# Retention and gated MLP on one core: state sums in SBUF for two chunks at a time, a two-step norm, other staging and a new order of the steps

## The chip, the cores and the metric

The kernel runs on 1 core of one Trainium2 chip. The metric is the device time in microseconds (us) of one execution; lower is better. The engines are TensorE (PE, with its weight loads shown as PEld), VectorE (DVE), ScalarE (ACT), GpSimd (POOL) and SyncE (SP, which here only issues DMAs). Each engine works through its own instructions in order; engines wait for each other by semaphores.

## The reference

Attention without softmax, with a decay that depends on the distance (retention), is followed by a gated MLP block whose gate mixes along the sequence (a 576 x 576 matrix `w_sg`). Batch 8, 8 heads, sequence 576, head size 64, model width 512, `d_ff` 1024.

```
scores = scale * q @ k^T
ret    = scores * where(rel >= 0, gamma_h ** rel, 0)      # per head
x      = (ret @ v) with the heads side by side             # [8, 576, 512]
h      = gelu_tanh(x @ w_in);  u, v = halves of h          # 512 columns each
v_n    = (v - mean(v)) / sqrt(var(v) + 1e-6) * g_ln
v_s    = w_sg @ v_n (along the sequence) + b_sg
out    = x + (u * v_s) @ w_out
```

## The kernel before

The 8 x 576 = 4608 rows are cut into 18 blocks j of 256 rows, each of two chunks of 128 rows, c or t = 0 and 1. In the attention part a block is held with two neighbouring rows on one partition: 64 partitions are chunk 0, 64 are chunk 1. Half of one chunk in nine belongs to the next batch (`m == MID`); there the states begin anew.

The whole program is one list of words, `ORDER`, written out by hand or by a tool; each word calls one step, and the steps are recorded in that order. Because every engine works in order, this list sets what stands ahead of what on PE, DVE, ACT, POOL and in SP's queue. A letter at the end of a word (A, D, P) gives the engine of an evacuation or a cast. A PSUM tag (x0, x1, w, y, z) gives the bank that a step writes; a step waits until the earlier content of its tag has been read. The steps, with their names in the list and in the trace:

- `ld:j:part` loads q, k or v of a block (`qf`, `kf`, `vf`), 512 KB each; `ldw` loads a weight, `ldg` the gain `g_ln`. All go through SP's queue.
- `cast` makes bf16 of them: `qb` = q times the decay of its row (two halves, L302), `kb` (two halves), `vb` = v times the inverse decay (L309).
- `T` transposes q or k on PE (`tp`, eight transposes, L327), `Te` copies the result to `qT` or `kT`. For 15 of the 36 a DMA transpose does it (`Td`).
- `Sc:j:g` makes the scores inside a chunk for half of the heads (`sc`, L350), `Sce` masks them (`ret`, DVE, L360).
- `Z:j:c` adds k^T v of one chunk to the state, in PSUM (`zp`, L382; 16 matmuls of 64 x 64): the running sum stays in one PSUM tile of a pool of its own (`psZ`) from one start of a batch to the next. `Ze` copies the sum to bf16 (`zb`), which later chunks read.
- `inter:j` and `intra:j` give the block's output (`ot`, L419): `ot<-qT,zb` from the states, `ot<-ret,vb` within the chunk. `intrae` copies it to `xT`, a ring of 9 blocks. Matmuls of 64 x 64 use one quarter of PE's array each; matmuls of different quarters run side by side.
- `V:j` makes the second half of h (`hv`, L454), `Ve` its GELU (`vg`); `mom` the mean and variance on DVE; `pow` the inverse root (`rs`) on POOL; `cen` on DVE `vc = (vg - mean) * g_ln` in one SCALAR_TENSOR_TENSOR (L484); `norm` `vn = vc * rs` on ACT, POOL or DVE (L498, L500; the chunk with two batches into two tiles `vnm`, always on ACT, L493).
- `U:j:x` and `Ue` make the first half of h (`hu`, L509; `uT`). `W:b:c:x` multiplies with the transposed `w_sg` (`wp`, L523), `We` multiplies with `uT` to `gT` (L528). `wT` and `wTe` are the transposes of `w_sg` for it; `sg` casts its rows to bf16 first, into a free part of `uT`.
- `O:j:t` multiplies with `w_out` (`op`, L535). The residual x is either added on PE (four matmuls with the identity, L538) or, for the six blocks with a word `xd` (a DMA transpose of `xT` to `xn`), by DVE in `Oe` (L547). `Oe` otherwise copies (`ob`), `st` stores.

Of the kernel before, what the change touches and what calls it, by code (L numbers as in the profile page):

```python
# [13 lines left out]
I32 = mybir.dt.int32  # L14
# [14 lines left out]
wTe:8:A ld:4:v:0 U:2:0:x0 cast:4:q:P norm:0:0:A T:4:q:x1 Ue:2:0 ld:4:v:1 Sce:3:1 Ze:3:1:A intra:3 mom:2:0 intrae:3:A cast:4:k:P ld:5:k Te:4:q:D
cen:1:0 norm:0:1:A cen:1:1 U:1:0:w norm:1:0:A T:4:k:x1 V:3:b:z Te:4:k:D ld:5:v Sc:4:0 U:2:1:x1 bd:0 Ue:1:0 pow:2:0 Ve:3:b cast:5:q:P mom:2:1  # L30
norm:1:1:A T:5:q:x0 Sce:4:0 cast:4:v:P ld:6:k:1 Te:5:q:A inter:4 Sc:4:1 U:3:0:w W:0:0:0:0:x0 Sce:4:1 intra:4 Z:4:1 mom:3:0 ld:6:q:1 Ue:2:1 cast:5:k:P
ldw:out ld:6:q:0 Ue:3:0 T:5:k:w intrae:4:A U:3:1:x1 cen:2:0 cen:2:1 V:4:b:z norm:2:0:A Te:5:k:D cast:5:v:P ld:6:v:1 Ue:3:1 Ze:4:1:D W:0:0:0:1 Sc:5:0
mom:3:1 ld:6:k:0 We:0:0:0 Z:5:0 Sce:5:0 Ze:5:0:A Ve:4:b W:0:3:0:2:w cast:6:q:P ld:7:q wc:out:A W:0:1:1:2:x1 ld:6:v:0 We:0:3:0 W:0:2:0:2:x0 We:0:2:0
inter:5 We:0:1:1 Sc:5:1 W:0:1:0:2:w W:0:2:1:2:x0 W:0:3:1:2:x1 Sce:5:1 We:0:2:1 We:0:1:0 intra:5 cast:6:k:P pow:2:1 Z:5:1 We:0:3:1 ld:7:k intrae:5:A
U:4:1:w T:6:q:x0 V:5:b:z cen:3:0 Ue:4:1 Ze:5:1:A cen:3:1 cast:7:q:P T:6:k:x1 mom:4:0 U:5:1:w ld:7:v Te:6:q:A W:0:0:1:0:x0 Te:6:k:A U:5:0:x1 Sc:6:0
norm:2:1:P cast:6:v:D mom:4:1 Z:6:0 Ve:5:b W:0:0:1:1 cast:7:k:P Ue:5:1 O:0:0:w We:0:0:1 Sce:6:0 mom:5:0 pow:3:b Ue:5:0 Ze:6:0:A O:1:1:x0 Z:6:1 inter:6
norm:3:0:D ld:8:q cast:7:v:P Td:7:q Oe:1:1:A Sc:6:1 Sce:6:1 ld:8:k Oe:0:0:A O:0:1:x0 norm:3:1:A T:7:k:x1 ld:8:v cen:4:1 mom:5:1 Ze:6:1:A Te:7:k:A
U:4:0:w bd:1 ld:9:q intra:6 Ue:4:0 Sc:7:0 pow:4:b intrae:6:A Z:7:0 Oe:0:1:A ld:9:k O:1:0:x1 cen:5:1 cen:4:0 ld:10:k Sce:7:0 V:6:b:z Ze:7:0:D
cast:8:k:A Ve:6:b cast:8:q:P pow:5:b Oe:1:0:A U:6:1:x0 norm:4:0:D T:8:k:w inter:7 Te:8:k:D Sc:7:1 cast:8:v:P Z:7:1 Sce:7:1 T:8:q:x1 Ue:6:1 cen:5:0
st:0 Ze:7:1:A W:1:3:0:2:w ld:9:v W:1:2:0:2:x0 Te:8:q:A We:1:2:0 intra:7 Sc:8:0 cast:9:k:P Z:8:0 norm:4:1:A Td:9:k W:1:0:1:2:x1 We:1:3:0 W:1:0:0:2:w  # L40
ld:11:k:0 W:1:1:0:2:x0 mom:6:0 We:1:0:1 norm:5:0:A We:1:0:0 intrae:7:A U:7:0:x1 Ue:7:0 V:7:b:z We:1:1:0 Ve:7:b O:2:1:x1 mom:6:1 cast:10:k:P ld:10:q
Oe:2:1:A Ze:8:0:D Sce:8:0 cast:9:q:P ld:11:q:0 mom:7:0 cast:9:v:P ld:10:v W:1:3:1:2:w inter:8 Sc:8:1 We:1:3:1 norm:5:1:P ld:11:q:1 Sce:8:1 mom:7:1
T:9:q:x1 U:6:0:w W:1:1:1:2:x0 We:1:1:1 Te:9:q:A Z:9:0 Ue:6:0 cen:6:1 cen:6:0 intra:8 intrae:8:A Sc:9:0 pow:6:b W:1:2:1:2:x1 norm:6:0:D cast:10:q:P
U:7:1:w V:8:b:z norm:6:1:A W:2:3:0:2:x0 pow:7:b Ue:7:1 Td:10:k We:1:2:1 Sce:9:0 ld:11:k:1 Ve:8:b Ze:9:0:A ld:11:v:1 cen:7:0 W:2:0:0:2:x1 U:8:1:w
cast:10:v:P We:2:3:0 Z:9:1 inter:9 Sc:9:1 Ue:8:1 mom:8:0 W:2:0:1:2:x0 T:10:q:w ld:13:k:1 We:2:0:0 Sce:9:1 norm:7:0:A Te:10:q:D W:2:3:1:2:x1 Ze:9:1:A
intra:9 st:1 Sc:10:0 Z:10:0 W:2:1:1:2:w We:2:3:1 We:2:0:1 Ze:10:0:A O:3:0:x1 intrae:9:A mom:8:1 cast:11:q:P ld:11:v:0 pow:8:b Sce:10:0 cast:11:k:A
We:2:1:1 cen:7:1 O:3:1:x0 V:9:b:z cen:8:1 Td:11:q U:8:0:w Oe:3:1:A Oe:3:0:A cen:8:0 Ve:9:b W:2:2:1:2:x1 norm:7:1:A mom:9:0 norm:8:0:P inter:10 Z:10:1
Sc:10:1 Ue:8:0 We:2:2:1 Ze:10:1:A O:2:0:x0 Oe:2:0:A W:2:2:0:2:x1 Sce:10:1 norm:8:1:P Td:11:k W:3:0:1:2:w W:2:1:0:2:x0 ld:12:q ld:13:q:0 intra:10
# [44 lines left out]
def kernel(  # L93
# [510 lines left out]
```

## Time and profile before

| | |
|---|---|
| time, median of 3 runs | 218.66 us (218.62 to 219.58) |
| the profiled execution: its own time | 218.48 us |
| its span, first to last instruction | 216.7 us |
| busy: PE, PEld, DVE, ACT, POOL | 194.7, 136.8, 170.3, 123.3, 122.1 us |
| instructions: DVE, ACT, POOL | 289, 179, 144 |
| granted TensorE clock | 1.00 |
| HBM read, written | 33.05 MB, 9.44 MB |

Busy time of an engine is the time in which at least one of its instructions runs. The matmul spans on PE overlap, so a step's cost there is read from start to start. In a row of groups stand line, engine, operation, out<-in with shapes and types, the count, then busy us and mean ns of one, then the engine's idle time just before them and what ended most of it.

### The profile page before, as it was taken

To read this page: it belongs to the slowest core of one execution; us is meant where nothing else is said; L and a number is where in the kernel's file an instruction comes from. 1 tells how busy PE (TensorE), PEld (TensorE's weight loads), DVE (VectorE), ACT (ScalarE), POOL (GpSimd) and SP (SyncE) were. 2 spreads that over 40 slices of the span, in tenths; PEclk is the share of its full clock that TensorE was granted. 3 is DMA by queue.
4 is the path that set the end of the run, shared out by engine and by line. 5 is a ranking of instruction groups with operands and counts; after the bars stand their busy time and mean duration, and the time that the engine had idled before them with its cause. 6 is when DMAs were issued, how large, how long until landed. Compare 5 with 4: busy or idle time off the path is not lost.

```text
span 216.7 us, 7228 instructions
## 1 busy us (share of the span) xinstructions
PE 194.7 (90%) x3101; PEld 136.8 (63%) x3130; DVE 170.3 (79%) x289; ACT 123.3 (57%) x179; POOL 122.1 (56%) x144
## 2 busy tenths in 40 slices
PE   0468788899999989999999999999999999999993
PEld 0355566577677657686667767686756675666751
DVE  3666858988995899799977678797988887977770
ACT  3356475697868578567563477833674457633102
POOL 5055338889169996988368565659729422151000
PEclk9999999999999999999999999999999999999999
DMA  6999999998999999999779899999899999450755
GB/s 168 290 343 355 222 233 263 208 226 190 290 217 254 208 247 324 197 249 174 184 172 282 180 263 252 217 207 254 128 269 230 265 238 271 141 149 3 191 198 194
DMA packets 86704, 48.47 MB, mean 224 GB/s; under 512 B 24528, under 2 KB 79824, under 8 KB 86672
## 3 DMA queue, kind: packets, MB, share of 16 engines
q1 hardware_dynamic: 86560, 48.00, 96.7%
q8 instruction: 24, 0.39, 0.8%
q14 instruction: 8, 0.07, 0.1%
q10 hardware_dynamic: 112, 0.00, 0.0%
HBM read 33.05 MB, written 9.44 MB: 196 GB/s over the span
## 4 chain that ended last, share of the span: by engine, by line
PE 63%; DVE 16%; DMA 12%; ACT 2%; issue 2%; SPq 1%; POOL 1%; DVEq 0%; ACTq 0%; POOLq 0%
PE wp L523 14%; PE op L535 12%; DMA vf<-in_v_dram 12%; PE hv L454 11%; PE hu L509 10%; PE ot L419 5%; DVE ret L360 5%; PE sc L350 3%; DVE vc L484 3%; PE zp L382 2%; DVE bst L468 2%; PE op L538 2%; DVE vn L500 2%; PE wtp L279 2%; PE tp L327 2%
## 5 line engine op out<-in xcount | busy, mean ns | idle before, releaser
L360 DVE TENSOR_TENSOR ret<-sc,mask 128x1024 bf16<-128x1024 f32 x36 | 43.8, 1216 | 5.8 <-PE sc L350 5.6
L302 POOL TENSOR_TENSOR qb<-qf,gq 128x512 bf16<-128x512 f32 x30 | 32.7, 1109 | 22.1 <-DMA qf<-in_q_dram 20.7
L523 PE MATMUL wp<-wT,vn 128*128 128x288 bf16 x256 | 40.8, 286 | 0.1
L509 PE MATMUL hu<-xT,w_in 128*128 128x256 bf16 x288 | 36.8, 273 | 0.0
L535 PE MATMUL op<-w_out,gT 128*128 128x512 bf16 x126 | 35.0, 380 | 1.2 <-issue 0.3
L528 DVE TENSOR_TENSOR gT<-wp,uT 128x288 bf16<-128x288 f32 x64 | 28.0, 449 | 9.8 <-PE wp L523 8.2
L454 PE MATMUL hv<-w_in,xT 128*128 128x512 bf16 x133 | 34.0, 382 | 1.6 <-ACT xT L137 0.8
L137 ACT CAST xT<-ot 128x1024 bf16<-128x1024 f32 x17 | 22.3, 1311 | 17.8 <-PE ot L419 17.7
L484 DVE SCALAR_TENSOR_TENSOR vc<-vg,mv,g_bc 128x512 f32<-128x512 f32 x36 | 31.5, 897 | 0.2
L514 ACT ACTIVATE uT<-hu 128x512 bf16<-128x512 f32 x36 | 21.3, 599 | 16.7 <-PE hu L509 16.4
L509 PEld LDWEIGHTS <-w_in 128*128 128x128 bf16 x288 | 27.1, 98 | 5.0
L523 PEld LDWEIGHTS <-vn 128*128 128x128 bf16 x256 | 24.6, 98 | 8.0 <-issue 0.4
L309 POOL TENSOR_TENSOR vb<-vf,gv 128x1024 bf16<-128x1024 f32 x13 | 25.1, 1934 | 7.2 <-DMA vf<-in_v_dram 5.5
L468 DVE BATCH_NORM_STATS2 bst<-vg 128x6 f32<-128x512 f32 x36 | 24.6, 683 | 4.5 <-ACT vg L461 4.5
L461 ACT ACTIVATE vg<-hv 128x1024 f32<-128x1024 f32 (+1 forms) x19 | 18.6, 980 | 13.2 <-PE hv L454 11.6
L500 POOL TENSOR_SCALAR vn<-vc,rs 128x512 bf16<-128x512 f32 x12 | 20.6, 1720 | 9.3 <-DVE vc L484 9.2
L454 PEld LDWEIGHTS <-xT 128*128 128x128 bf16 x144 | 13.5, 99 | 14.7 <-ACT xT L137 1.4
L137 ACT COPY ob<-op 128x512 f32<-128x512 f32 x20 | 11.5, 586 | 18.5 <-PE op L538 17.8
L477 POOL TENSOR_SCALAR rs<-mv 128x2 f32<-128x2 f32 (+1 forms) x19 | 8.1, 427 | 23.8 <-DVE mv L469 22.8
L535 PEld LDWEIGHTS <-gT 128*128 128x128 bf16 x144 | 12.9, 98 | 11.6
L523 PE MATMUL wp<-wT,vnm 128*128 128x288 bf16 x64 | 18.0, 287 | 0.3 <-DVE kT L137 0.3
L350 PE MATMUL sc<-qT,kT 64*64 64x128 bf16 x576 | 16.3, 223 | 0.8 <-DVE ret L360 0.6
(74 smaller groups left out, 283.2 us busy)
## 6 DMA issues: line engine op xcount, KB each, us to landing
out_dram<-ob SPq DMA_DIRECT2D x16, 512.0 KB, 4.6
kf<-in_k_dram SPq DMA_DIRECT2D x12, 512.0 KB, 7.6
qf<-in_q_dram SPq DMA_DIRECT2D x12, 512.0 KB, 6.6
vf<-in_v_dram SPq DMA_DIRECT2D x12, 512.0 KB, 8.1
gT<-in_moe_w_in_dram SPq DMA_DIRECT2D x2, 1024.0 KB, 9.5
qf<-in_q_dram SPq DMA_DIRECT2D x4, 384.0 KB, 8.2
kf<-in_k_dram SPq DMA_DIRECT2D x4, 384.0 KB, 8.3
vf<-in_v_dram SPq DMA_DIRECT2D x4, 384.0 KB, 8.5
```

The costliest lines, as they stand in the source:

```text
L137: (nc.scalar.copy if eng == "A" else ENG[eng].tensor_copy)(o, i)
L302: ENG[eng].tensor_tensor(s["qb"][:, a], paired(x)[:, a], g, op=Alu.mult)
L309: ENG[eng].tensor_tensor(s["vb"][:].rearrange("p a h d -> p h a d"), x[:], bc(gv, j), op=Alu.mult)
L360: nc.vector.tensor_tensor(s["ret"][:, :, 2 * g:2 * g + 2].rearrange("p r x a t -> p r x (a t)"), PS.pop(("Sc", j, g))[:].rearrange("p r x ...
L454: nc.tensor.matmul(hv[:, n], xT[:, (2 * j + t) % (2 * RING), kk, :], w_in[:, kk, F2:], start=(kk == 0), stop=(kk == KK - 1))
L468: nc.vector.bn_stats(bst[:], s["vg"][:, t])
L484: nc.vector.scalar_tensor_tensor(s["vc"][:, t], s["vg"][:, t], s["mv"][:, t, 0:1], g_bc[:], op0=Alu.subtract, op1=Alu.mult)
L500: ENG[eng].tensor_scalar(vn[:], vc[:, t], rs[:, t:t + 1], None, op0=Alu.mult)
L509: nc.tensor.matmul(hu[:, i, :], w_in[:, kk, 128 * c:128 * c + 128], xT[:, c0:c0 + 2, kk, :], start=(kk == 0), stop=(kk == KK - 1), skip_gr ...
L523: nc.tensor.matmul(PS["W", b, c, x][:], vns[t0 + j][e][:, 128 * c:128 * c + 128], wT[:, e, j, x * HS:(x + 1) * HS], start=(j == 0), stop=( ...
L528: nc.vector.tensor_tensor(gT[:, c, col:col + HS], PS.pop(("W", b, c, x))[:], uT[:, c, col:col + HS], op=Alu.mult)
L535: nc.tensor.matmul(op[:], gT[:, c, 128 * i:128 * i + 128], w_out[:, c, :], start=(c == 0), stop=(c == KK - 1 and not turn), skip_group_che ...
```

## The change

**States.** `psZ` is gone; its bank becomes a fourth rotating tag (v) beside x0, x1 and w. `Z:j:0` only takes a PSUM slot; `Z:j:1` then issues the matmuls of both chunks, interleaved, each chunk into its own slot (in 14 blocks; blocks 4, 8, 13 and 17 have one state addition, as before). `Ze` no longer copies a running sum: it adds the chunk's product from PSUM to the sum of the chunk ahead, f32 in SBUF (`zs`), always on DVE (24 words), or copies it where a state begins (8 words). A new word `Zc` casts `zs` to `zb`: 12 on ACT, 5 on DVE, 15 on POOL.

**Norm.** For blocks 0 to 15, `cen` and `norm` are replaced by `xh` and `gm`. `pow` makes one more small value per chunk on POOL (`mr` = -mean * rs). `xh` makes the normalised row, `vc = vg * rs + mr`, as one ACT activation with two per-row operands (30 words), or on DVE (2); `gm` multiplies with `g_ln` to `vn`, a TENSOR_TENSOR of two SBUF operands, 17 on DVE and 15 on POOL (two halves for the chunk with two batches). Blocks 16 and 17 keep `cen` and `norm`.

**Staging.** The bf16 rows of `w_sg` go to tiles that share the buffers of `ob` and `xn` (`wpad`), no longer to `uT`; the last 64 rows of `w_sg` are loaded by a word of their own (`s5`). Some small tables share buffers too.

**Head.** `fill:n:tag` puts n matmuls of zeros (128 x 512) on PE: ten words, 33 matmuls, the last ahead of `intra:1`.

**End.** The last unit, `O:17:1`, is computed, copied and stored in two halves of 256 columns (`Oh`, `Oeh`, `sth`).

**Turns and order.** T words 21 to 23, `Td` 15 to 13, `xd` 6 to 8 blocks; all words stand in a new order, with other engines for many evacuations and casts. Words per engine (before to after): `Oe` ACT 20 to 16, DVE 16 to 19; `Te` ACT 12 to 14, DVE 9 and 9; q casts DVE 3 to 5, POOL 15 to 13; k casts ACT 7 to 9, DVE 2 to 0; `intrae` ACT 17 to 15, DVE 1 to 3; `wTe` ACT 4 to 6, DVE 6 to 4.

The core of the diff (of the list the first line alone):

```
-ld:0:k rl ld:0:q ld:0:v cast:0:k:D ld:1:k T:0:k:x1 ld:1:q mk:0 cast:0:q:D Te:0:k:A T:0:q:x1 cast:0:v:D Z:0:0 Te:0:q:A Ze:0:0:A mk:1 Sc:0:0 Z:0:1
+warm rl ld:0:q ld:0:k cast:0:q:P ld:0:v fill:10:v T:0:q:x0 cast:0:k:A mk:0 T:0:k:v ldw:v cast:0:v:D ld:1:q mk:2 mk:1 Te:0:q:A ld:1:k Te:0:k:A spare
...
-    psZ = ctx.enter_context(tc.tile_pool(name="psZ", bufs=1, space=bass.MemoryType.PSUM))
...
+    def fill(n, tag):
+
+        o = ps2("idle", [128, 4, 128], tag)
+        for _ in range(n):
+            nc.tensor.matmul(o[:], zeros[:], zeros[:].unsqueeze(1).to_broadcast([128, 4, 128]), start=True, stop=True,
+                             skip_group_check=True)
...
+    def Z_mm(j, c, tag):
+
+        s = blk[j]
+        PS["Z", j, c] = ps2("zp", [128, KK, D], tag)
+        if c == 0 and (2 * j + 1) % NT != NT - 1:
+            return
+        for part in (False, True):
+            rows = [[], []]
+            for c in range(2):
+                if ("Z", j, c) not in PS or ((2 * j + c) % NT == MID) != part:
+                    continue
+                lo = slice(64 * c + (32 if part else 0), 64 * c + 64)
+                for a in range(2):
+                    for kk in range(KK):
+                        for r in range(2):
+                            rows[c].append((r, 64, lambda z=PS["Z", j, c], lo=lo, a=a, kk=kk, r=r: nc.tensor.matmul(
+                                z[half(r), kk, :], s["kb"][lo, a, kk, r, :], s["vb"][lo, a, hd(r, kk), :],
+                                start=(a == 0 and kk == 0), stop=True, skip_group_check=True)))
+            interleave(rows)
...
+    def Z_out(j, c, eng):
+
         i = 2 * j + c
...
+        sums[i] = w2.tile([128, KK, D], F32, name="zs")
+        z = PS.pop(("Z", j, c))
+        if opens(i):
+            move(eng, sums[i][:], z[:])
+        else:
+            nc.vector.tensor_tensor(sums[i][:], z[:], sums[i - 1][:], op=Alu.add)
+
+    def Z_cast(j, c, eng):
+        i = 2 * j + c
+        zbs[i + 1] = w3.tile([128, KK, D], BF, name="zb")
+        move(eng, zbs[i + 1][:], sums[i][:])
...
+        if j < NB - 2:
+            for t in tiles(t):
+                nc.gpsimd.tensor_scalar(blk[j]["mr"][:, t:t + 1], blk[j]["mv"][:, t, 0:1], blk[j]["rs"][:, t:t + 1], -1.0,
+                                        op0=Alu.mult, op1=Alu.mult)
+
+    def unit(j, t, eng):
...
+            nc.scalar.activation(s["vc"][:, t], s["vg"][:, t], Act.Identity, bias=s["mr"][:, t:t + 1],
+                                 scale=s["rs"][:, t:t + 1])
...
+    def gain(j, t, eng):
...
+            ENG[eng].tensor_tensor(vn[:], vc[:, t], g_bc[:], op=Alu.mult)
```

How the list moves the instructions is shown at three places. First SP's queue, from its first DMA on; a tile's name is followed by the array it is loaded from. Before:

```order
L158 DMA kf<-in_k_dram 128x8x128
L158 DMA qf<-in_q_dram 128x8x128
L158 DMA vf<-in_v_dram 128x8x128
L158 DMA kf<-in_k_dram 128x8x128
L158 DMA qf<-in_q_dram 128x8x128
L201 DMA gT<-in_moe_w_in_dram 128x4x512
L158 DMA vf<-in_v_dram 128x8x128
L201 DMA gT<-in_moe_w_in_dram 128x4x512
L201 DMA gT<-in_moe_w_sg_dram 128x4x576
```

SP's queue now, from its first DMA on:

```order
L160 DMA qf<-in_q_dram 128x8x128
L160 DMA kf<-in_k_dram 128x8x128
L160 DMA vf<-in_v_dram 128x8x128
L223 DMA gT<-in_moe_w_in_dram 128x4x512
L160 DMA qf<-in_q_dram 128x8x128
L160 DMA kf<-in_k_dram 128x8x128
L160 DMA vf<-in_v_dram 128x8x128
L160 DMA kf<-in_k_dram 96x8x128
```

q stands ahead of k in block 0, one half of `w_in` ahead of block 1, and all of block 1 ahead of the other half; the second half of `w_in` has moved behind block 2 and `w_sg` behind block 3.

Second DVE in the first block, from the v cast (`vb`) to the second masked score (`ret`). Before:

```order
L309 TENSOR_TENSOR vb<-vf,gv 128x8x2x64
L246 TENSOR_SCALAR mask_137<-rel 128x256
L249 MEMSET mask_137 32x4x16
L360 TENSOR_TENSOR ret<-sc,mask_136 128x2x512
L246 TENSOR_SCALAR mask_138<-rel 128x256
L249 MEMSET mask_138 32x4x16
L360 TENSOR_TENSOR ret<-sc,mask_136 128x2x512
```

DVE now, from the masks of the first block to the q cast of the second; `zs` is the state's f32 sum:

```order
L267 MEMSET mask_135 32x4x16
L139 COPY zs<-zp 128x256
L378 TENSOR_TENSOR ret<-sc,mask_134 128x2x512
L418 TENSOR_TENSOR zs<-zp,zs 128x256
L378 TENSOR_TENSOR ret<-sc,mask_134 128x2x512
L320 TENSOR_TENSOR qb<-qf,gq 128x512 x2
L139 CAST xT<-ot 128x8x2x64
```

The state's copy and its sum, one of them on ACT before, stand ahead of the two `ret`; a q cast and the copy to `xT`, on POOL and ACT before, stand behind them.

Third POOL in the middle, around the casts of blocks 7 and 8. Before:

```order
L137 CAST kb<-kf 128x512 x2
L477 TENSOR_SCALAR rs<-mv 128x2
L478 TENSOR_TENSOR rs<-rs,mhalf 128x2
L309 TENSOR_TENSOR vb<-vf,gv 128x8x2x64
L477 TENSOR_SCALAR rs<-mv 128x2
L478 TENSOR_TENSOR rs<-rs,mhalf 128x2
L302 TENSOR_TENSOR qb<-qf,gq 128x512 x2
```

POOL now, around the same casts; `vn<-vc,g_bc` is a gain product, `zb<-zs` a state's cast:

```order
L139 CAST kb<-kf 128x512 x2
L327 TENSOR_TENSOR vb<-vf,gv 128x8x2x64
L535 TENSOR_TENSOR vn<-vc,g_bc 128x512 x2
L139 CAST zb<-zs 128x256
L320 TENSOR_TENSOR qb<-qf,gq 128x512 x2
L327 TENSOR_TENSOR vb<-vf,gv 128x8x2x64
L139 CAST zb<-zs 128x256
```

Two gain products and two state casts have come between the input casts of block 7 and those of block 8; each state cast waits for what stands ahead of it.

More of the change, by code (lines that the diff above doesn't have):

```diff
@@ L29 @@
[L29 to L36, printed above, removed]
@@ L364, in Sc_out, with opens @@
             op=Alu.mult)
-    zcur = [None]
-    def Z_mm(j, c):
+    def opens(i):
+        return i % NT in (0, MID)
+    def Z_mm(j, c, tag):
         s = blk[j]
-        i = 2 * j + c
-        m = i % NT
-        first = m in (0, MID)
-        if first:
-            zcur[0] = psZ.tile([128, KK, D], F32, name="zp")
-        z = zcur[0]
-        lo = slice(64 * c + (32 if m == MID else 0), 64 * c + 64)
-        rows = [[], []]
-        begun = set()
-        def mm(a, kk, r):
-            h = hd(r, kk)
-            nc.tensor.matmul(z[half(r), kk, :], s["kb"][lo, a, kk, r, :], s["vb"][lo, a, h, :],
-                             start=(first and r not in begun), stop=True, skip_group_check=True)
-            begun.add(r)
-        for a in range(2):
-            for kk in range(KK):
-                for r in range(2):
-                    rows[c].append((r, 64, lambda a=a, kk=kk, r=r: mm(a, kk, r)))
-        interleave(rows)
-        PS["Z", j, c] = z
```

187 lines of the change are left out of this document (121 added, 66 removed).

## The prediction

> **What bounds the kernel now.** I read first the busy times by stage (length; then busy time and count of PE, PE weight loads, DVE, ACT, POOL; granted clock; DMA share; GB/s):
>
> ```profile
> 0.00:15.00 15.00, 4.61 (x84) 3.42 (x85) 8.07 (x23) 6.83 (x10) 5.01 (x18) 1.00 0.94 263
> 15.00:45.00 30.00, 25.17 (x483) 18.16 (x486) 22.47 (x36) 18.20 (x27) 19.10 (x32) 1.00 1.12 258
> 45.00:104.00 59.00, 57.37 (x1002) 41.82 (x1008) 53.46 (x81) 42.46 (x60) 46.88 (x48) 1.00 1.11 236
> 104.00:213.00 109.00, 107.48 (x1535) 73.39 (x1552) 86.34 (x152) 55.27 (x82) 51.12 (x48) 1.00 0.89 204
> ```
>
> PE stands idle 10.4 + 4.8 = 15.2 us before 45, and 1.6 + 1.5 = 3.1 in the 168 us after it. So two things shorten this kernel: fewer idle microseconds in the head, or less PE work. Relief of DVE, ACT or POOL after 45 buys at most those 3.1. The chain that ended last says the same: in the head it goes over DVE, near the end from one PE group straight into the next (start, us, what):
>
> ```profile
> 9.45 1.24 DVE vb L309
> ...
> 13.80 1.24 DVE ret L360
> 15.08 1.28 PE ot L419 x36
> ...
> 85.87 0.25 PE zp L382 x16
> ...
> 199.05 2.59 PE op L535 x12
> 201.64 0.87 PE hu L509 x8
> ```
>
> As marks of progress I take the starts of `ot<-ret`, the attention product of a block, in PE's timeline (block 0 at 15.08, above; blocks 1, 2 and 4 here):
>
> ```profile
> 5.55 1.03 PE L327 MATMUL tp<-ident,kb 128*128 128x128 bf16 x8 [5.55 <-DVE kb L137]
> ...
> 23.85 0.64 PE L419 MATMUL ot<-ret,vb 64*64 64x128 bf16 x32 [1.32 <-DVE ret L360]
> ...
> 38.65 0.64 PE L419 MATMUL ot<-ret,vb 64*64 64x128 bf16 x32
> ...
> 53.37 0.64 PE L419 MATMUL ot<-ret,vb 64*64 64x128 bf16 x32
> ...
> 121.16 0.61 PE L327 MATMUL tp<-ident,qb 128*128 128x128 bf16 x8
> ```
>
> The first and last rows are the same eight transposes: 1.03 us in the head, 0.61 later, though the granted clock is 1.00 in both stages.
>
> **Term 1, state additions of both chunks at once.** In 14 blocks two groups of 16 pairs on half of PE's tiles become one group of 32 on all four. One group of 16 costs 0.25 (row at 85.87), 15.6 ns a pair. If the tiles run side by side, 32 pairs cost 0.25 as well and 14 x 0.25 = 3.5 us of PE work go; if PE can't take pairs faster, nothing goes. How fast pairs can come shows where state additions, `ot` and `sc` of different tiles mix:
>
> ```profile
> 121.86 0.24 PE L419 MATMUL ot<-qT,zb 64*64 64x128 bf16 x1
> ...
> 122.01 0.20 PE L419 MATMUL ot<-qT,zb 64*64 64x64 bf16 x2
> ```
>
> 13 matmuls start in these 0.15 us: 11.5 ns a pair, a merged group of 0.37, 14 x (0.50 - 0.37) = 1.8 us saved. That rate may still be limited by the tiles, so I take 2.3, nearer to it than to 3.5: **-2.3 us (-3.5 to 0)**.
>
> The Trainium skill (TensorE: Matmul & The Clock Gate, section "Wait — 56ns, not 53.3ns?") speaks against this part: starts of small matmuls never come closer than about 25 ns, by which merging would buy nothing. The trace differs, with 15.6 and 11.5 ns.
>
> **Term 2, transposes and residuals.** T words go from 21 to 23, at most 0.54 each (0.61 with the last one's run-out, row at 121.16). Blocks whose residual is added outside PE go from 6 to 8, which saves four groups like this:
>
> ```profile
> 211.57 0.39 PE L538 MATMUL op<-ident,xT 128*128 128x128 bf16 x4
> 211.79 1.03 PE L535 MATMUL op<-w_out,gT 128*128 128x512 bf16 x4
> ```
>
> Start to start 0.22, so 4 x 0.22 = 0.9 against 1.1: **0 (-0.2 to +0.2)**. There are 21 DMA transposes before (15 + 6) and after (13 + 8).
>
> **Term 3, the head.** Durations of what moves (in the groups by line: busy, mean ns):
>
> ```profile
> L302 POOL TENSOR_TENSOR qb<-qf,gq 128x512 bf16<-128x512 f32 x30 | 32.7, 1109 | 22.1 <-DMA qf<-in_q_dram 20.7 <-issue 1.1 <-PE zp L382 0.3
> L484 DVE SCALAR_TENSOR_TENSOR vc<-vg,mv,g_bc 128x512 f32<-128x512 f32 x36 | 31.5, 897 | 0.2
> L528 DVE TENSOR_TENSOR gT<-wp,uT 128x288 bf16<-128x288 f32 x64 | 28.0, 449 | 9.8 <-PE wp L523 8.2 <-ACT uT L514 0.9 <-issue 0.2
> L500 POOL TENSOR_SCALAR vn<-vc,rs 128x512 bf16<-128x512 f32 x12 | 20.6, 1720 | 9.3 <-DVE vc L484 9.2
> L137 POOL CAST kb<-kf 128x512 bf16<-128x512 f32 x18 | 12.0, 693 | 3.3 <-DMA kf<-in_k_dram 3.1 <-ACT wT L137 0.2
> L498 ACT ACTIVATE vn<-vc,rs 128x512 bf16<-128x512 f32 x15 | 10.7, 722 | 2.2 <-POOL rs L478 1.2 <-DVE vc L484 1.0
> L137 ACT CAST zb<-zp 128x256 bf16<-128x256 f32 x26 | 9.7, 372 | 10.5 <-PE zp L382 10.4
> L302 DVE TENSOR_TENSOR qb<-qf,gq 128x512 bf16<-128x512 f32 x6 | 3.9, 690 | 2.3 <-DMA qf<-in_q_dram 2.3
> ```
>
> A state sum on DVE reads PSUM and SBUF like `gT`: 449 for 288 columns, about 0.41 for 256. Block 0: v still lands for a cast at 9.45; cast 1.24, merged group 0.3, then on DVE sum 0.41, `ret` 1.24, sum, `ret`: 9.45 + 1.24 + 0.3 + 3.3 = 14.3, 0.8 before 15.08. Block 1 on DVE after that: q cast 1.4, `xT` 1.3, split of b 1.2, v cast 1.2, `qT` 0.7, two sums and two `ret` 3.3: 23.4, 0.5 before 23.85. Block 2: first group statistics follow, a q cast, the w_in cast; then V of block 1 (1.7) and four U (3.5) run on PE: about 33 against 38.65. But all ten w_sg transposes (4.1 by two in 0.82), done there before, are still to come, against one U and one T more: 5.6 earlier with 2.8 of work postponed, a lead of 2.8. Block 4: about 47.2 against 53.37, 2.2 postponed, a lead of 4.0. Then the loads step in: up to q of block 5 the new order carries 11.8 MiB, 12.3 MB, and the slices (5.42 us each) reach that in the ninth, at 48 us:
>
> ```profile
> GB/s 168 290 343 355 222 233 263 208 226 190 290 217 254 208 247 324 197 249 174 184 172 282 180 263 252 217 207 254 128 269 230 265 238 271 141 149 3 191 198 194
> ```
>
> A DVE cast of 1.4 puts its transposes at 49.5 to 50, where PE would be there at about 48.5: one microsecond of lead goes. So **-3.0 us (-5.5 to 0)**; a loss here would need more work ahead of the mark of block 4, and DVE, which the chain runs over, has as much there as before (four `vc`, three `wT` and some casts less; seven sums, two q casts and two `xT` more). The 33 fill matmuls are on nothing's way: each stands where PE waits for a load, a cast or a `ret`, and keeps the clock up (0.61 instead of 1.03); that gain is in the 0.3 and the T's above. Without that cover each costs 0.22 (2.59 / 12 for matmuls of that size, row at 199.05), 7.1 in all.
>
> **Term 4, the other engines after 45 us.** DVE loses 32 `vc` (32 x 0.90 = 28.7) and five `vn`; it gains 17 gain products (two SBUF inputs to bf16, like `qb`: 0.69, bounds 0.69 and 0.90), 24 sums (0.41), five state casts, two unit norms, and net one or two casts and evacuations of each kind: about 6 us less of 170. ACT loses 22 `zb` (8.2) and 16 `vn` words, gains 30 unit norms (like `vn`, 0.72), 12 state casts and more casts: about +5 on 123. POOL loses twelve `vn` (20.6) and gains 15 gain products (like `qb`, 1.11; three are in two halves), 15 state casts (half of `kb`, 0.35), 32 small `mr` (0.23 each or more), the w_in cast: about +11 on 122. None becomes longer than PE. Who waits behind whom changes: `zb` was one ACT step out of PSUM (0.37), now a DVE sum and a cast (0.41 + 0.35 to 0.41), on POOL behind casts of 1.1 to 2.2. PE has 4 to 6 us of other groups between a merged addition and its reader from block 7 on, so I let the 3.1 idle us grow a little: **+0.7 (-1.0 to +8)**. The two-step norm is hidden by the same distance to W.
>
> **Term 5, the end.**
>
> ```profile
> 213.08 0.59 ACT L137 COPY ob<-op 128x512 f32<-128x512 f32 x1 [0.46 <-PE op L538]
> 213.69 0.33 SPq L561 DMA_DIRECT2D out_dram<-ob  x1
> ```
>
> Half a unit instead of 0.59 saves about 0.2, the smaller last store (3.0 from its issue to the end of the span) some more: **-0.4 (-0.1 to -0.7)**.
>
> **Sum.** -2.3 + 0 - 3.0 + 0.7 - 0.4 = -5.0. The profiled execution took 218.48 (span 216.7 and 1.8 around it), 0.18 below the median 218.66; so 213.5 for it, **213.7 us** as a median. The lowest ends together give 218.66 - 10.9 = 207.8.
>
> **Rivals.** I count 0.5%, 1.1 us, as what a measurement here can tell from no change.
>
> *Loads set the pace* (15%): the lead of Term 3 is eaten whole, since the DMA share is already 1.1 from 15 to 104 us; Term 1 gives its 1.8. 218.66 - 1.8 - 0.4 = 216.5. Against: PE waited on ACT and DVE in the marks above, not on loads.
>
> *The additions don't merge* (8%): PE takes pairs at 15.6 ns whatever the tiles. Without 2.3: 216.0. For: `ot` on four tiles (row at 23.85) runs 32 pairs in 0.64, no faster. Against: the 11.5 ns.
>
> *It does what it says but comes out even* (9%): Terms 1 and 3 at 0, about 218.3.
>
> *Slower: DVE and POOL in each other's way* (15%). Operations on DVE that read two SBUF operands, or could run fast, are long when POOL works (min/median/max):
>
> ```profile
> L484 DVE SCALAR_TENSOR_TENSOR vc<-vg,mv,g_bc x36: 719/744/2158, 40.6 to 197.8; 128x512 f32<-128x512 f32 x36
> L500 DVE TENSOR_SCALAR vn<-vc,rs x5: 478/1369/2147, 73.2 to 200.6; 128x512 bf16<-128x512 f32 x5
> ```
>
> There are fewer such on DVE now (17 gain products for 36 `vc` and five `vn`), but POOL is fuller, and the states that `inter` reads sit behind its queue in six blocks (3, 7, 11, 12, 14, 16). With 1.4 us of extra wait in each, 8.4 us: 218.66 - 5.0 + 8.4 = 222.1. It decides from 5.0 / 6 = 0.8 us a block. Against: the cover of 4 to 6 us. The Trainium skill (SBUF — State Buffer, section "Who interferes with whom") has this as a lock: a DVE operation with two SBUF inputs and a POOL one that reads SBUF exclude each other. The 719 to 2158 above agree.
>
> *Forecast* (53%): 213.7, its own range 209.5 to 216.
>
> **How the numbers follow.** Faster: forecast 53 + loads 15 + no merging 8 = 76%; within 0.5%: 9%; slower: 15%. The range must leave out 2 in 10: above, the slow rival (15%) and a little of the even one; below, some 4% of the forecast's own tail. 208.0 to 219.5.
>
> **What would show it.** Right: `ot<-ret` of block 4 near 47 and of block 5 near 60; PE without gaps after that; a merged `zp` group of 32 in 0.25 to 0.4; DVE busy near 164, POOL near 133. Wrong: block 4 after 51 (loads), `zp` groups of 0.5 (no merging), PE waiting for `zb` from POOL for more than 3 us in all, or POOL above DVE in busy time.

## The result and the profile after

After: 221.84 us median of 4 runs (220.98 to 223.0); before beside them 218.64 (218.62 to 219.58). The ratio is 1.013, 95% interval 1.009 to 1.017: 1.3% slower, where 2.3% faster was forecast. The profiled execution took 221.68 (span 219.9) against 218.48. Ratios leave out runs with a disturbed granted clock and medians hold them, so the two can differ.

The changed kernel by the four stages (length; busy time and count of PE, PE weight loads, DVE, ACT, POOL; clock; DMA share; GB/s):

```profile
0.00:15.00 15.00, 11.97 (x108) 5.10 (x109) 7.34 (x23) 6.84 (x11) 10.38 (x34) 0.89 0.98 264
15.00:45.00 30.00, 25.23 (x511) 16.71 (x514) 24.13 (x40) 19.42 (x30) 15.79 (x22) 1.00 1.18 253
45.00:104.00 59.00, 55.91 (x977) 40.64 (x985) 52.09 (x87) 44.36 (x61) 47.26 (x60) 1.00 0.99 227
104.00:213.00 109.00, 106.27 (x1522) 72.12 (x1538) 85.78 (x153) 56.87 (x83) 61.41 (x80) 1.00 0.96 202
```

PE is fuller up to 15 us only because of the fills. After 45 it stands 3.1 + 2.7 = 5.8 us, before the change 1.6 + 1.5 = 3.1. DVE's busy time is as before, not 6 us less. The marks of progress, `ot<-ret` of blocks 0, 1, 2 and 4 in PE's timeline:

```profile
15.01 0.64 PE L447 MATMUL ot<-ret,vb 64*64 64x128 bf16 x32
23.47 0.64 PE L447 MATMUL ot<-ret,vb 64*64 64x128 bf16 x32 [0.34 <-DVE ret L378]
34.79 0.64 PE L447 MATMUL ot<-ret,vb 64*64 64x128 bf16 x32
...
52.35 0.64 PE L447 MATMUL ot<-ret,vb 64*64 64x128 bf16 x32
```

Block 4 has a lead of 1.0 us over before (53.37), with 2.2 of work postponed by the prediction's estimate: 1.2 behind in work. What PE waited for in the changed kernel (us in total, times, longest):

```profile
PE tp L345 <- POOL qb L320: 2.7, 4, 1.0
PE wtp L297 <- issue: 1.5, 1, 1.5
PE wp L581 <- DVE zs L418: 1.3, 1, 1.3
...
PE zp L403 <- POOL vb L327: 0.9, 1, 0.9
```

First and last stand for loads: POOL had been waiting for q or v. (Of the 2.7 us, 1.6 fall in block 0, at 6 and 7 us, and e13, which has its loads in time, waits 1.7 there too. Ahead of the v cast of block 2 at 23.91 the changed kernel's profile names ACT's copy to `kT`; with large pieces the same cast starts at 19.2 to 19.9, before that copy, so the load is what it lacked.) The third is one place, at 59 us. The second has no releaser in the profile.

### The profile page after: what moved, and what is told of

It reads as the page before. It is cut to its first block, busy times and chain, and to the rows that moved or that the text cites. A ratio compares the mean times of both kernels' runs of the same rounds, so it can differ in the third digit from the quotient of the medians.

```text
span 219.9 us, 7349 instructions
## 1 busy us (share of the span) xinstructions
PE 202.6 (92%) x3138; PEld 136.5 (62%) x3167; DVE 171.8 (78%) x303; ACT 127.9 (58%) x183; POOL 134.8 (61%) x194
## 3 DMA queue, kind: packets, MB, share of 16 engines
q1 hardware_dynamic: 86704, 48.01, 97.5%
## 4 chain that ended last, share of the span: by engine, by line
PE 51%; DMA 14%; DVE 13%; SPq 9%; POOL 5%; issue 3%; ACT 2%; DVEq 0%; ACTq 0%; POOLq 0%
PE wp L581 12%; DMA qf<-in_q_dram 11%; PE hu L567 9%; PE op L593 9%; PE hv L482 8%; SPq L160 7%; PE ot L447 4%; DMA out_dram<-ob 3%; DVE ret L378 3%; POOL qb L320 3%; PE sc L368 3%; DVE vn L535 2%; PE wtp L297 2%; PE tp L345 2%; PE zp L403 2%
## 5 line engine op out<-in xcount | busy, mean ns | idle before, releaser
L567 PE MATMUL hu<-xT,w_in 128*128 128x256 bf16 x288 | 35.9, 273 | 0.0
L320 POOL TENSOR_TENSOR qb<-qf,gq 128x512 bf16<-128x512 f32 x26 | 27.5, 1080 | 13.4 <-DMA qf<-in_q_dram 12.6
L593 PE MATMUL op<-w_out,gT 128*128 128x512 bf16 x126 | 33.6, 379 | 0.9 <-DVE ob L605 0.2
L482 PE MATMUL hv<-w_in,xT 128*128 128x512 bf16 x129 | 33.0, 380 | 1.3 <-DVE xT L139 0.5
L139 ACT CAST xT<-ot 128x1024 bf16<-128x1024 f32 x15 | 19.7, 1314 | 14.3 <-PE ot L447 14.3
L518 ACT ACTIVATE vc<-vg,mr,rs 128x512 f32<-128x512 f32 x30 | 24.1, 813 | 0.1
L482 PEld LDWEIGHTS <-xT 128*128 128x128 bf16 x144 | 13.3, 98 | 14.6 <-DVE xT L139 0.6
L505 POOL TENSOR_SCALAR rs<-mv 128x2 f32<-128x2 f32 (+1 forms) x19 | 5.6, 292 | 24.0 <-DVE mv L497 23.0
L506 POOL TENSOR_TENSOR rs<-rs,mhalf 128x2 f32<-128x2 f32 (+1 forms) x19 | 16.0, 843 | 1.6
L368 PE MATMUL sc<-qT,kT 64*64 64x128 bf16 x576 | 15.5, 220 | 1.5 <-DVE ret L378 0.7
L535 POOL TENSOR_TENSOR vn<-vc,g_bc 128x512 bf16<-128x512 f32 x12 | 16.0, 1344 | 0.0
```

Source lines behind the costliest of these rows:

```text
L320: ENG[eng].tensor_tensor(s["qb"][:, a], paired(x)[:, a], g, op=Alu.mult)
L368: nc.tensor.matmul(o, s["kT"][half(r), a, kk, half(c)], s["qT"][half(r), :, kk, half(c)], start=True, stop=True, skip_group_check=True)))
L482: nc.tensor.matmul(hv[:, n], xT[:, (2 * j + t) % (2 * RING), kk, :], w_in[:, kk, F2:], start=(kk == 0), stop=(kk == KK - 1))
L518: nc.scalar.activation(s["vc"][:, t], s["vg"][:, t], Act.Identity, bias=s["mr"][:, t:t + 1], scale=s["rs"][:, t:t + 1])
L567: nc.tensor.matmul(hu[:, i, :], w_in[:, kk, 128 * c:128 * c + 128], xT[:, c0:c0 + 2, kk, :], start=(kk == 0), stop=(kk == KK - 1), skip_gr ...
L593: nc.tensor.matmul(op[:], gT[:, c, 128 * i:128 * i + 128], w_out[:, c, :], start=(c == 0), stop=(c == KK - 1 and not turn), skip_group_che ...
```

## The experiments

Each kernel ran beside the kernel before, so the ratio to before is what compares them. Order words are as in the listing.

**e1: no fills.** All ten `fill` words are taken out.

> The changed kernel without its 33 fill matmuls. Fills in the way (the row of six takes 2.7 us cold, 0.43 each, ahead of the state additions of block 0): block 0's ot<-ret starts at 14.1 instead of 15.0, block 4 up to 1 us earlier, the whole 220.8 to 221.3. Fills pay by the clock: transposes and scores stay at 1.0 instead of 0.55 us past 12.8, block 4 later than 52.4, the whole 223 or more. Loads set the pace (q of block 2 lands at 25.9 whatever PE did before): block 2 at 34.8 and block 4 at 52.4 as before the edit, the whole 221.8 within 0.5.

Ratio 1.0215 (1.018 to 1.026), 223.9 us: no faster without them. Against 1.013, and 1.0176 when the changed kernel ran again (e11), it is not clear that they pay. In the way they are, at one place: block 0's `ot<-ret` comes at 14.19 without them and at 15.01 with them. In the changed kernel six cold fills stand straight ahead of block 0's state additions:

```profile
8.22 2.70 PE L172 MATMUL idle<-zeros 128*128 128x512 bf16 x6
10.86 0.76 PE L403 MATMUL zp<-vb,kb 64*64 64x64 bf16 x32
```

By block 1 nothing is left of it (23.50 and 23.47). Block 4 comes later without fills, at 54.30. The clock of this run is shown in the last section.

**e2: norm in one step from block 2 on.**

```diff
-xh:j:t:A ... gm:j:t:D (or :P)
+cen:j:t  ... norm:j:t:A (or :P)
```

> The changed kernel with the norm in one step again from block 2 on: (vg - mean) x gain on DVE where the unit norm stood on ACT, the product with rs on ACT where the gain product stood on DVE and on POOL where it stood there; the small mr products of blocks 2 to 15 are gone. Two-step norm to blame (gain products and POOL's products lock each other out, the 1.4 us wait at 59.0 goes): 218 to 220. Not to blame: DVE gets 28 products of 0.75 to 0.9 and loses 14 of 0.69 to 1.5, so 221.5 to 224.

Ratio 1.0447 (1.040 to 1.050): in this order the two-step norm as a whole is worth about 3%, and isn't the cause.

**e3: POOL's state casts on ACT** (15 times `Zc:j:c:P` to `Zc:j:c:A`).

> The changed kernel with the 15 state casts of POOL on ACT instead, at the same places. State chain behind POOL's queue to blame: the waits of PE for zb and of the blocks behind it go, 219.5 to 220.8. Not to blame (PE never waited for zb from POOL in the trace): 221.8 within 0.8, ACT's queue taking as much as POOL's gave.

Ratio 1.0168 (1.011 to 1.023): not better. That half of the slower rival, states behind POOL's queue, finds no support.

**e4: the two chunks' additions one after the other.**

```diff
-        for part in (False, True):
+        for only in range(2):
...
-                if ("Z", j, c) not in PS or ((2 * j + c) % NT == MID) != part:
+                if ("Z", j, c) not in PS or c != only:
...
```

> The changed kernel with the two chunks' state additions issued one after the other, everything else in place: the price of merging alone. If merging takes 2 us of PE work away (0.25 instead of two times 0.25 to 0.37 in 10 blocks) and PE's work sets the time: 223.4 to 224.5. If PE waits for others often enough to hide it: 221.8 to 222.6.

Ratio 1.0116 (1.007 to 1.016): merging buys nothing that shows. Block 5 in PE's timeline, merged (the changed kernel):

```profile
57.55 0.42 PE L368 MATMUL sc<-qT,kT 64*64 64x128 bf16 x16
57.85 0.45 PE L403 MATMUL zp<-vb,kb 64*64 64x64 bf16 x32
58.23 1.05 PE L567 MATMUL hu<-xT,w_in 128*128 128x256 bf16 x8
```

and one after the other (e4):

```profile
57.50 0.42 PE L368 MATMUL sc<-qT,kT 64*64 64x128 bf16 x16
57.75 0.57 PE L403 MATMUL zp<-vb,kb 64*64 64x64 bf16 x32
58.25 1.05 PE L567 MATMUL hu<-xT,w_in 128*128 128x256 bf16 x8
```

From the scores to `hu` it is 0.68 against 0.75: 0.07 saved, where the forecast had 2.3 / 14 = 0.16. The 32 pairs start within 0.25 us in the first case and within 0.38 in the second: one after the other the two groups overlap too, since they use different tiles, and 0.05 goes again because the merged group starts later behind the scores.

**e5, b4: blocks 0 to 5 in large pieces**, in the changed kernel and in the one before; **e6, b5: all blocks; e10: blocks 6 to 17 in the changed kernel.**

```diff
+                if j < 6:   # b5, e6: 18; e10: j > 5
+                    flat_rows = src.rearrange("b h s d -> (b h s) d").rearrange("(n p a) d -> n p (a d)", p=128, a=2 * H)
+                    nc.sync.dma_start(dst[p0:p1].rearrange("p h a d -> p (h a d)"), flat_rows[j, p0:p1])
+                    continue
```

> The changed kernel with q, k and v of blocks 0 to 5 read in pieces of 4 KB in place of 512 bytes: the same bytes, queue and order, but from other places, so that the values of the first blocks are others. Loads to blame for the lost head: PE's waits of 1.3 us at 24.6 and 1.5 at 41.8 go, block 4's ot<-ret starts by 49.5 (52.3 in the changed kernel), the whole 218 to 219.5. Loads not to blame: block 4 after 51.5, the whole within 0.8 of 221.8.

> The kernel before with the same edit of its loads (values of the first blocks are others). If the order before already had its loads in time, block 4 stays at 52.5 to 53.4 and the whole at 217.8 to 219; if loads set its pace too, block 4 comes 2 us or more earlier and the whole is 215 to 217.

> The changed kernel with q, k and v of all 18 blocks read in pieces of 4 KB (the same bytes; the values are others). If the loads took the whole forecast gain: 214 to 216, PE's waits for qb gone. If the rest of the loss after 48 us is the order's own (waits of state additions, norms and slots for one another): 217 to 219, as with blocks 0 to 5 alone.

> The kernel before with q, k and v of all blocks read in pieces of 4 KB (the values are others). Its order had its loads in time: 218 to 220, no different from 218.6 to 219.8. If loads hold it as well: 215 to 217.

> The changed kernel with only blocks 6 to 17 read in pieces of 4 KB (their values are others). With blocks 0 to 5 alone the ratio to before was 0.995, with all 0.990, unchanged 1.013. If head and later loads add up: 1.008. If the later loads cost as much by themselves: 1.000 to 1.004.

Changed kernel: e5 0.995 (0.991 to 0.998), e10 1.002 (0.997 to 1.006), e6 0.990 (0.986 to 0.993). Kernel before: b4 1.000 (0.997 to 1.003), b5 1.003 (0.999 to 1.007). Loads in time are worth 2.3% to the new order and nothing to the old one. (In the profile of b4 block 4 does not stay at 52.5 to 53.4 but comes at 56.64, with a granted clock of 0.72 from 40 to 46 us; the whole is the same even so.) But e6, at 217.31 us, lies in the second range of its expectation: late loads did not take the whole forecast gain. The head's loads take 1.8% of it (e5), the later ones 1.1% (e10); they don't quite add up. The DMA queue of the changed kernel (packets, MB, share of 16 engines' span):

```profile
q1 hardware_dynamic: 86704, 48.01, 97.5%
```

and of e6, the same bytes:

```profile
q1 hardware_dynamic: 38320, 48.01, 81.1%
```

**e7: e6 with the additions one after the other**, as in e4.

> The same with the two chunks' state additions one after the other: what merging is worth where PE waits less for loads. By the prediction's first term: 2.3 (1.8 to 3.5) above the run with all loads in large pieces. By the group rows of the run with split additions (0.07 to 0.15 saved for each of 10 groups): 0.7 to 1.5 above it, or not above it at all.

Ratio 0.9915 (0.988 to 0.995) against 0.9898: 0.4 us for merging, with about 1.1 of uncertainty either way.

**b1, b2: one part in the order before.** b1 puts `Z:j:0` and `Z:j:1` side by side with `Ze` on DVE and `Zc` where the evictions stood; b2 replaces `cen` and `norm` by `xh` and `gm`.

> The kernel before, its order kept, with the merged state additions alone: both chunks' pairs at once where the first chunk's stood, sums in SBUF on DVE, casts where the evictions stood. By the prediction's first term with nothing lost: 216.4 (215.2 to 218). If a merged group saves only 0.1 us against its neighbours, as the run with split additions says, and the sums load DVE: 218.5 to 221.

> The kernel before, its order kept, with the two-step norm alone (unit norm on ACT where the centering stood or behind the power, gain product where the norm stood, on the engines that the changed kernel uses; statistics of blocks 2 and 3 taken to the power a little earlier). If the two-step norm costs by itself (gain products and POOL's in each other's way): 220 or more. If it is free or helps: 217.5 to 219.2.

Ratios 1.062 (1.055 to 1.070) and 1.061 (1.057 to 1.065): both far over what was expected. In either, PE waits at more than a dozen places. They show that the parts can't be priced one by one in an order not made for them, and not what each is worth in the new one.

**b6: the order before with 28 fills and the last unit halved.**

> The kernel before, its order kept, with 28 fill matmuls in the waits of PE up to 25 us and with the last unit in two halves: the two parts of the change that lean on no other. If fills get PE to full clock before 12 us and the transposes of blocks 0 and 1 shorter: block 0 0.5 us earlier, the whole 0.5 to 1.5 faster than before. If the head goes at the pace of DVE and ACT: the whole within 0.5 of before, the half unit 0.2 to 0.5 of it.

Ratio 1.002 (0.999 to 1.005): nothing from the two together. Block 0 comes 1.4 us earlier (13.71), and block 4 no earlier (53.44 against 53.37): what is won at the start of the old order is lost again by block 4.

**e8, e9: two steps moved behind loads in SP's queue.**

```diff
-Td:8:k ld:9:q ... ld:11:k:1 ... ld:9:k ld:9:v
+ld:9:q ld:9:k ld:9:v Td:8:k ... ld:11:k:1          (e8 and e9)
-bd:0 ... ld:6:k:1 ldw:out ld:6:k:0
+ld:6:k:1 ldw:out ld:6:k:0 bd:0                     (e9)
```

They follow from two views of the changed kernel: SP's queue,

```profile
73.88 0.53 SPq L160 DMA_DIRECT2D vf<-in_v_dram  x1
79.53 1.34 SPq L355 DMA_TRANSPOSE kT<-kb  x1
80.97 0.52 SPq L160 DMA_DIRECT2D qf<-in_q_dram  x1
...
87.33 1.34 SPq L160 DMA_DIRECT2D qf<-in_q_dram  x1
```

and PE at 96 us:

```profile
96.84 0.40 PE L345 MATMUL tp<-ident,qb 128*128 128x128 bf16 x4 [0.44 <-POOL qb L320]
97.85 0.40 PE L345 MATMUL tp<-ident,qb 128*128 128x128 bf16 x4 [0.62 <-POOL qb L320]
```

SP issues nothing for 5.1 us, since the transpose in front waits for its cast; the loads of blocks 9 to 11 stand behind it, and the q issued at 87.33 is the one that PE's transposes at 96.8 lack. In the same way `bd:0` waits 3.0 us at 47.3 for ACT's copy to `wT`, with the loads of block 6 behind it:

```profile
46.89 0.44 SPq L160 DMA_DIRECT2D vf<-in_v_dram  x1
50.35 1.88 SPq L284 DMA_DIRECT2D wT<-parts  x3
52.33 0.54 SPq L160 DMA_DIRECT2D kf<-in_k_dram  x1
```

> The changed kernel with the DMA transpose of k of block 8 behind the loads of q, k and v of block 9 in SP's queue (they stand ahead of it now, and ahead of a piece of block 11). If SP's queue standing for 5.1 us at 74.4 makes block 9 and 10 late: q of block 10 lands 3 to 5 us earlier, PE's waits of 0.62 and 0.78 at 96 to 97 go, the whole 0.8 to 1.8 faster than the changed kernel. If the loads are late by their rate alone: within 0.5 of it.

> The same, and the rows of b that go to wT (bd:0) behind the loads of k of block 6 and of w_out. If the queue standing for 3.0 us at 47.3 matters too: another 0.5 to 1.5 faster, PE's wait of 1.4 at 59.0 shorter or gone. If not: as with the transpose alone, or slower where the rows come too late for the first wp group at 60.

e8: 1.0153 (1.008 to 1.023), no gain. The waits at 96 are gone, but the transpose itself now comes late:

```profile
87.21 0.42 PE L368 MATMUL sc<-qT,kT 64*64 64x128 bf16 x16 [1.62 <-DMA kT<-kb]
```

e9: 1.004 (0.999 to 1.010). A gain against 1.013 to 1.018 is likely, but it rests on six runs.

**e11: the changed kernel again.**

> The changed kernel once more, unchanged, beside these runs: 1.013 times before by the first comparison (1.009 to 1.017). By the clock it may vary: where the record shows half clock for 3.4 us behind a wait of PE, the run is 1 to 2 us longer.

Ratio 1.0176 (1.011 to 1.024), the first result within its interval.

**e12: e9, and one gain product moved from POOL to DVE** (`gm:1:1:P` to `gm:1:1:D`); **e13: the same with all loads in large pieces.**

> The changed kernel with the two queue steps behind the loads (as e9) and the gain product of block 1's second half on DVE in place of POOL. In e9 DVE's two 64-row products of block 2 take 3.23 us while POOL multiplies beside them (vn 1.72), and PE waits 1.4 us at 59.5 for what stands behind them. If the two engines lock each other out: the two products take 1.4 to 2.4, PE's wait falls below 0.7, the whole 0.5 to 1 below e9 (1.000 to 1.003 times before). If the products are slow by themselves (64 rows): they stay at 3 us, DVE is 0.7 later still, the whole as e9 or slower.

> The same with q, k and v of all blocks in pieces of 4 KB (their values are others). If late loads, the standing queue and this lock are all that kept the changed kernel from its forecast, less the 2 us that merging doesn't bring: 215 to 216, 0.980 to 0.987 times before. If large pieces had already taken away what the two queue steps cost: 0.988 to 0.991 as with large pieces alone.

DVE of the changed kernel at 57 us, and POOL beside it:

```profile
57.09 2.94 DVE L531 TENSOR_TENSOR vnm<-vc,g_bc 64x512 bf16<-64x512 f32 x2
60.06 0.42 DVE L418 TENSOR_TENSOR zs<-zp,zs 128x256 f32<-128x256 f32 x1
```

```profile
55.42 2.38 POOL L327 TENSOR_TENSOR vb<-vf,gv 128x1024 bf16<-128x1024 f32 x1
57.76 1.72 POOL L535 TENSOR_TENSOR vn<-vc,g_bc 128x512 bf16<-128x512 f32 x1
```

and DVE of e12:

```profile
56.71 1.60 DVE L536 TENSOR_TENSOR vn<-vc,g_bc 128x512 bf16<-128x512 f32 x1
...
58.61 1.37 DVE L532 TENSOR_TENSOR vnm<-vc,g_bc 64x512 bf16<-64x512 f32 x2
60.01 0.98 DVE L419 TENSOR_TENSOR zs<-zp,zs 128x256 f32<-128x256 f32 x2
```

The two products halve when POOL's product is away: DVE and POOL do hold each other up. But DVE is not done earlier. The product that came over takes 1.60 beside POOL's v cast, together 2.97 against 2.94, and the state sum behind starts at 60.01 instead of 60.06. e12 is at 1.007 (1.004 to 1.011), no better than e9, and PE now waits 0.9 us for the rows of b, which come too late. With loads in time, e13 is at **0.978 (0.973 to 0.983)**, 214.64 us against 219.71: 5.1 us faster. It is no kernel to keep, since it reads other values. It stands 1.2% under e6, with intervals that don't touch, so the queue steps and the moved product together count once the loads are in time; which of them does is not shown. Its PE, from block 4 on:

```profile
51.30:104.00 52.70, 52.70 (x982) 38.47 (x982) 47.84 (x86) 42.76 (x59) 40.77 (x52) 1.00 0.69 222
```

No idle time at all there; in the changed kernel PE stands 2.7 us in the same stretch. No version that computes the reference beat the kernel before.

## Why the prediction was wrong, point by point

**Term 1 (forecast -2.3): mis-sized.** A merged group does start its pairs in 0.25 to 0.28 us in ten of the blocks, as foreseen, but in the four blocks where a sequence's middle tile falls it is issued in two parts and takes 0.6. And the price of a group is not from its first start to its last: it ends when the next group starts. By that it saves 0.07 to 0.15 in each of the ten, 0.7 to 1.5 us in all; e7 against e6 measured 0.4 (±1.1). That the Trainium skill (TensorE: Matmul & The Clock Gate, "Wait — 56ns, not 53.3ns?") would have had merging buy nothing comes near the result, though not by its rule: 31 starts in 0.25 us are 8 ns apart, not 25.

**Term 2 (0).** Not tried alone; nothing in the trace speaks against it.

**Term 3 (-3.0): the step that failed.** The walk by durations held up to block 1 (14.3 and 23.4 forecast, 15.01 and 23.47 measured; block 0 at 14.30 in e4, whose cold fills ended sooner, and at 14.19 without fills), and broke at block 2, 34.79 for 33: v of block 2 held PE to 25.9. I had let the loads in only at block 5, by bytes moved until 48 us at the pace of before. That sum was wrong in two ways. The new queue puts 512-byte packets ahead of the weights' longer rows, so less has landed early: the GB/s row of the changed kernel's page has 211 in the fourth slice, where before it had 355. By 22 us that is some 0.7 MB less; by 33 us the two are level.

```profile
GB/s 171 337 288 211 302 302 263 194 225 141 266 213 288 189 133 264 251 223 303 235 218 215 195 214 281 139 205 121 245 234 224 350 107 241 167 148 143 151 230 194
```

And the order before had work without loads for PE there, the w_sg transposes that the new one postpones.

Late loads are not all that the walk had wrong. Of the 5.2 us missing at block 4 (52.35 for 47.2), 1.8 were missing at block 2 and 3.4 came after it. From block 1's mark to block 2's the changed kernel takes 11.32 us, and 9.85 to 9.86 with large pieces (e5, e6, e13), near the 9.6 of the forecast: there 1.5 us are the loads'. But from block 2's mark to block 4's the forecast had 14.2, and in the changed kernel, e5, e6 and e13, in this order, it took (columns as in the first fence):

```profile
34.79:52.35 17.56, 14.71 (x296) 9.98 (x296) 13.10 (x20) 11.99 (x20) 12.14 (x20) 1.00 1.13 207
31.61:47.92 16.31, 14.61 (x296) 9.91 (x297) 12.90 (x20) 11.98 (x20) 14.44 (x24) 1.00 0.68 186
33.29:50.46 17.17, 14.61 (x295) 9.90 (x296) 13.10 (x20) 11.99 (x20) 16.10 (x25) 1.00 0.59 156
33.56:51.27 17.71, 14.70 (x297) 9.90 (x296) 13.11 (x20) 11.97 (x20) 15.53 (x24) 1.00 0.88 240
```

PE is busy for 14.6 to 14.7 us there, more than the walk gave the whole stretch, whatever the loads. The rest is nearly all waits: 1.2 to 1.3 us for `xT`, `ret` and statistics in each, and one among the w_sg transposes without a releaser, of 1.46, 0.20, 1.07 and 1.62 us. So with loads in time block 4 comes at 50.46 (e6) and 51.27 (e13), not at 47.2. That e5 has it at 47.92 is in part luck: its six fills ahead of block 0 took 1.46 us instead of 2.70, and its wait without a releaser is the short one. "The 33 fill matmuls are on nothing's way" failed at block 0, which they held up by 0.8 us (e1): there they cost 0.45 each (2.70 / 6), not the 0.22 of the prediction.

**Term 4 (+0.7): mis-sized.** PE's idle time from block 4's mark to 213 grew from 3.1 to 5.5 us. I walked DVE, ACT and POOL, but of SP's queue I only counted the transposes; that `bd:0` and `Td:8:k` wait there for other engines, with loads behind them, was nowhere in the sum. DVE came to 171.8, not 164, mostly since its gain products took 0.97, and 1.46 each for the two of 64 rows, instead of 0.69 (groups by line: busy, mean ns):

```profile
L535 POOL TENSOR_TENSOR vn<-vc,g_bc 128x512 bf16<-128x512 f32 x12 | 16.0, 1344 | 0.0
L535 DVE TENSOR_TENSOR vn<-vc,g_bc 128x512 bf16<-128x512 f32 x16 | 15.5, 967 | 0.0
...
L531 DVE TENSOR_TENSOR vnm<-vc,g_bc 64x512 bf16<-64x512 f32 x2 | 2.9, 1463 | 0.0
```

I took 0.69 for a product like `qb` when the rows that I quoted for the slower rival had the same kind at 719 to 2158. POOL (134.8) and ACT (127.9) came as forecast.

**Term 5 (-0.4).** The last matmul starts 3.1 later than before and the end 3.2: nothing gained. b6 does not speak against that.

**Sum.** Block 4 behind by 1.2 in work, 2.4 more of idle time after it, 0.4 less for merging: +3.2, and the profiled executions differ by 3.2. That it closes so well is partly luck: the 1.2 rests on an estimate, and the 0.4 is known to ±1.1 only.

**The rivals.** *Loads set the pace* (15%, 216.5) had the mechanism, with a price that was too low: I let the loads eat the lead and stop there. They cost 2.3% (e6 against the result), and after block 4 they go on costing. The sign was in view: a DMA share over 1.0 from 15 to 104 us. *Slower: DVE and POOL in each other's way* (15%, 222.1) had the time almost exactly and for the most part another cause: the casts behind POOL's queue cost nothing that shows (e3); that products on DVE and POOL slow each other is there, as the Trainium skill has it (SBUF — State Buffer, "Who interferes with whom"), and shows in PE's waits at one place, for 1.3 us. That e13 comes out 5.1 us faster, next to the forecast of 5.0, is no proof of the terms. Term 1 has hardly a part in it, and its profile (215.88 against 218.48) has the gain where the forecast had none: block 4 leads by 2.1 us, no more than the work postponed, and from there to the last matmul PE is idle for 0.4 us instead of 3.1.

Open: why PE waits 1.5 us among the w_sg transposes at 42 (no releaser; 0.20 in e5, 1.62 in e13); how the loads' loss splits between the packets' rate and the standing queue, which take partly the same waits.

## What to carry to other kernels

When a new order moves work that needs no loads behind work that does, walk the load queue like an engine: what is issued when, what each step ahead of a load waits for, and at which rate packets of that size land. A DMA share near 1 is a reason to do so, not yet a verdict: the order before had it too, and lost nothing to its loads (b5). Check each stretch of such a walk against the engine's own work in it. Price a group of small matmuls from the start of the group before it to the start of the one behind it. A DMA that needs an engine's result holds up the loads behind it in the queue; moved behind them it can make its own reader wait (e8), so look at both.

## What the runs showed of the hardware

**Packets.** 48,384 packets fewer for the same 48.0 MB took DMA from 97.5% of 219.9 us to 81.1% of 215.6 on 16 engines: 214.4 - 174.8 = 39.6 us each, 13 ns for every packet saved (an estimate from the two rows; the pieces also come from other places, and the two aren't told apart). The Trainium skill (DMA: Bandwidth & Descriptors, "Specifications") gives 512 bytes as enough for line rate; here pieces of 4 KB moved the same bytes in 18% less of the engines' time.

**The clock.** e1 by stretches (columns as in the first fence), where PE waits 1.6 us for v of block 2 (24.2 to 25.8) and is busy for 1.48 of the 3.5 us in the first row:

```profile
22.00:25.50 3.50, 1.48 (x62) 1.20 (x52) 2.04 (x4) 2.32 (x3) 1.65 (x1) 0.97 1.11 284
25.50:29.00 3.50, 2.95 (x42) 2.20 (x43) 2.50 (x5) 1.38 (x3) 0.91 (x3) 0.50 1.15 317
29.00:32.40 3.40, 3.40 (x26) 1.38 (x25) 1.32 (x3) 1.00 (x2) 3.30 (x5) 0.54 1.04 256
32.40:34.00 1.60, 1.60 (x26) 1.26 (x27) 1.60 (x3) 1.04 (x4) 1.60 (x3) 1.00 0.97 324
```

The granted clock halves for some 6.8 us, and block 2 comes at 37.06 instead of 34.79. The Trainium skill (TensorE: Matmul & The Clock Gate, "Why this matters for your kernels") warns of idle gaps over some 3 us; here the clock fell with no gap above 1.6 us in the 10 us ahead. That the wait brought it on is not shown. In the kernel before, PE was busy for even less ahead of block 1's product, with 1.3 us as its longest wait, and the clock stayed:

```profile
20.35:23.85 3.50, 1.39 (x73) 1.12 (x73) 2.50 (x3) 3.09 (x3) 0.00 (x0) 1.00 1.08 304
23.85:34.00 10.15, 9.51 (x123) 7.04 (x124) 7.38 (x19) 6.12 (x10) 5.22 (x6) 1.00 1.18 231
```

So a late load may cost a second price behind its wait, and when it does stays open.
